# A fifth exponent buffer, half the descriptor scratch, and one product moved ahead of the last attention values

## The chip, the core and the metric

The program runs on one core of a Trainium2 chip. A core has five engines that run their own instruction streams and meet through semaphores: TensorE (PE, with weight loads shown as PEld), VectorE (DVE), ScalarE (ACT), GpSimd (POOL) and SyncE (SP, which only issues transfers). The metric is the device time of one execution in microseconds, lower is better. Small differences matter here: about 0.2% of the time is what a measurement of this kernel can tell from no change.

## The reference

The computation is a soft-capped attention followed by a mixture of experts with one expert per token.

```
scores = scale * np.matmul(q, k.transpose(0, 1, 3, 2))      # 8 batches, 12 heads, 448 x 64
scores = cap * np.tanh(scores / cap)
attn = np.exp(scores); attn = attn / attn.sum(-1)
x = (attn @ v).transpose(0, 2, 1, 3).reshape(3584, 768)
expert = argmax(x @ w_gate)                                 # one of 8 for each token
out[token] = gate * relu(x[token] @ w1[expert]) @ w2[expert]
```

## The kernel before

**Attention.** The work is cut into 24 quads (8 batches of 3 quads; a quad is 4 heads), each quad into 7 tiles of 64 keys, and two tiles make a step, so there are 84 steps. In step k PE makes the scores of tiles 2k and 2k+1 into PSUM tiles `sp` (L255, two buffers). ACT takes a tanh of each into one half of an exponent tile `pt` (L265), and one step later makes the exponent of the whole tile in place (`expo`, L272). Three steps after the scores PE multiplies the exponents with the values into PSUM tiles `po` (`pv`, L322; `values` decides which tiles). DVE adds the exponents up for the denominators (`adds`, L277, into `acc` and then `p4`; `p4` shows as p in the trace), and when a quad is complete it copies its two `po` tiles to SBUF (`outp`, L329, tile `ot`). A quad has two `po` tiles and there are two buffers in all, so the first value product of a quad waits for the copies of the quad before. A quad has 7 tiles and a step has 2, so every other quad ends on the first tile of a step; then the second tile's value product is held back to the next step (`held`).

**What follows a batch.** Three steps after a batch's last step PE makes the sums of `p4` (`sums`, L349), later the gate logits (L349 too, from `ot`), the spread of the reciprocals (L398), and the counts of the routing (L430, L491, L493); DVE does the small steps between (`st`, `rec`, `lt`, `lr`, `ob`), and POOL stores rows and token lists in DRAM (`xd`, `ids`).

**The early block.** When three batches are routed, a first block of 448 tokens (block number -2) is collected during attention: POOL gathers its rows `xg` (L745), DVE scales (L890) and transposes them (L901, tile `xt`), POOL splits each of the six 128-row pieces into a high part `xh` (L908) and a low part `xl` (L909), and the first weight chunks are split too. Its first product, `up_mm(-2, 0)` (L940, 18 matmuls, PSUM tile `ph`), stands behind the last scores. `ph` lies in the PSUM banks that the score tiles `sp` had.

**Experts.** After attention, 8 blocks of tokens follow the early one: six large ones (448 tokens) and two small ones. For each, PE makes the products with w1 (`up`, L940) and w2 (`down`, L975 and L983); POOL gathers the rows of the next block and scatters those of the last one with indirect transfers (L745, L755), two weight chunks of each kind included.

**Order.** The order on each engine is written out by hand: the step loop, a table of tasks by step (`at`, `do`), and the code behind the loop. Every engine runs its instructions strictly in that order. Tiles come from pools with a number of buffers; an instruction that writes a buffer again waits for the last readers of it. The transfers that POOL issues need descriptors in an SBUF scratch of `RING` bytes in each partition; pool `pb` (which holds `pt`) is placed behind it, and some tiles of the later pool `hw` reuse the space of `pb`.

The end of attention is this code:

Of the kernel before, what the change touches and what calls it, by code (L numbers as in the profile page):

```python
# [4 lines left out]
F32 = mybir.dt.float32  # L5
# [10 lines left out]
B, H, S, D = 8, 12, 448, 64  # L16
# [7 lines left out]
QB = S // 32  # L24


RING = 4096
QN = 11
QR = QB - QN

# [96 lines left out]
def attention_moe(tc, qT, kT, vL, capd, wgL, w1a, w1b, w2a, w2b, cst, cmk, out):  # L127
# [13 lines left out]
    pb = pools("pb")  # L141
# [103 lines left out]
    pts = {}  # L245
# [14 lines left out]

    def tanh(t):
        if t % 2 == 0:
            pts[t // 2] = pb.tile([128, 2, 2, S], F32, name="pt", bufs=4)
        scale = qsc if t < KT else 1.0
        A.activation(out=pts[t // 2][:, t % 2], in_=sps.pop(t)[:, :, 0:S], func=AF.Tanh, scale=scale)  # L265

# [4 lines left out]
    def expo(k):  # L271
        A.activation(out=pts[k], in_=pts[k], func=AF.Exp, scale=capt)  # L272
# [40 lines left out]
    def pv(t):  # L313
        m, g = divmod(t, KT)
        vr = vrs[m]
        if g == 0:
            pvs[m] = [ps_o.tile([128, 512], F32, name="po", bufs=2) for _ in range(2)]
        pt = pts[t // 2][:, t % 2]
        for c in range(2):
            for j in range(2):  # L320
                r, w = slice(64 * c, 64 * c + 64), slice(64 * j, 64 * j + 64)
                PE.matmul(  # L322
                    pvs[m][c][w, 0:S], vr[r, g, j, :], pt[r, j, :], start=g == 0, stop=g == KT - 1
                )
# [412 lines left out]
    def width(j):  # L737
        return LARGE if large(j) else SMALL
# [65 lines left out]
    def high(i, f, e=A):  # L804
        w, r = ((w1s, w1r), (w2s, w2r))[i - 1]
        (e.copy if e is A else e.tensor_copy)(out=w[f][0], in_=r[f // 4][:, f % 4, :])
# [122 lines left out]
    def up_mm(j, f, r=None):  # L929
        r = r or slice(0, width(j))  # L930
        xh, xl = m["xh"], m["xl"]
        wh, wl = w1s[f]
        if (j, f) not in phs:
            phs[j, f] = m["ps_h"].tile([128, 512], F32, name="ph")[:, 0 : width(j)]
        ph = phs[j, f][:, r]
        i = 0
        for k in range(KC):
            c = slice(128 * k, 128 * k + 128)
            for w, x in ((wh, xh), (wh, xl), (wl, xh)):
                PE.matmul(ph, w[:, c], x[:, k, r], start=i == 0, stop=i == 3 * KC - 1)  # L940
                i += 1
# [154 lines left out]
    for k in range(KC):  # L1096
        t = n_first + 24 + 3 * k
# [17 lines left out]
    def values(k):  # L1115
        nonlocal held
        last = None
        ready = held + [2 * k - 6, 2 * k - 5]
        held = [ready.pop()] if ready[-2] % KT == KT - 1 else []
        for t in ready:  # L1120
            pv(t)
            if t % KT == KT - 1:
                last = t // KT
        return last

    for k in range(STEPS):
        for n in range(QUADS - 2):
            if k == (KT * (n + 1) - 1) // 2 + 1:
                load(n + 2, 1)
                if n + 3 < QUADS:  # L1130
                    load(n + 3, 0)
        for t in (2 * k, 2 * k + 1):
            scores(t)
            tanh(t)
        do(k, "act")
        if k >= 1:
            expo(k - 1)
        if k >= 3:
            last = values(k)
            if last is not None:  # L1140
                outp(last)
        do(k, "pe1")
        do(k, "v0")
        if k >= 2:
            adds(k - 2)
        do(k, "v1")
        do(k, "v")
        if k == STEPS - 3:
            room()
            split_w1(1, G, G)  # L1150
# [3 lines left out]
    m["ps_h"] = pools("ps_h", bufs=2, space=PSUM, side="right", **tw)  # L1154
    m["ps_z"] = pools("ps_z", space=PSUM, side="right", **tw)
    expo(STEPS - 1)
    assert values(STEPS) is None
    up_mm(-2, 0)
    high(1, 2)
    low(1, 2, G)  # L1160
    adds(STEPS - 2)
# [289 lines left out]
```

## Time and profile before

| | us |
|---|---|
| median of 3 runs | 805.44 (804.15 to 806.04) |
| the profiled execution | 804.61 |
| its span, first to last instruction | 802.7 |
| PE busy in the span | 780.4 (97%) |
| DVE, ACT and POOL busy | 551.7, 449.4 and 411.4 |

The profiled execution is 1.9 us longer than its span, and 0.8 us shorter than the median of the runs. A busy PE is not a PE at its peak, since matmuls overlap and their ends are modelled.

### The profile page before, as it was taken

The page shows a single profiled execution, that of the slowest core. Times are in us where ns is not written, and L with a number is a line of the kernel's source. Part 1 is how long each engine was busy: PE and PEld are TensorE (multiplying, and loading weights), DVE is VectorE, ACT ScalarE, POOL GpSimd, SP SyncE. Part 2 cuts the span into 40 slices and gives each one's busy share as a digit, 9 for nine tenths or more (in the row PEclk, how much of TensorE's full clock was granted, in tenths as well). Part 3 has the DMA queues.
Part 4 walks back from the last instruction along what each step waited for, and adds up shares of the span by engine and source line. Part 5 has one row for each costly group of instructions (what it writes and reads, how often), then busy time and mean ns, then how long its engine had stood idle before and what let it go on. Part 6 is the DMA issues. An engine that isn't in the chain of part 4 may idle for free.

```text
span 802.7 us, 15069 instructions
## 1 busy us (share of the span) xinstructions
PE 780.4 (97%) x5984; PEld 571.4 (71%) x5984; DVE 551.7 (69%) x908; ACT 449.4 (56%) x534; POOL 411.4 (51%) x400
## 2 busy tenths in 40 slices
PE   8999999999999989999999999999999999999995
PEld 3343434343434436899999999999999999999995
DVE  2788897998899997878549448358347357357730
ACT  7999999999998992343334324224224233234520
POOL 1001330318474465353785784884884884764742
PEclk9999999999999999999999999999999999999998
DMA  8325573488879602493441133542510252454211
GB/s 283 102 107 162 118 210 129 116 228 208 236 171 254 187 17 58 81 345 112 165 172 41 51 109 140 212 135 109 218 50 31 67 183 98 173 190 165 71 57 52
DMA packets 37102, 112.62 MB, mean 140 GB/s; under 512 B 8609, under 2 KB 15699, under 8 KB 34464
## 3 DMA queue, kind: packets, MB, share of 16 engines
q0 software_dynamic: 18528, 63.93, 25.5%
q1 hardware_dynamic: 18208, 47.43, 19.0%
q8 instruction: 49, 0.80, 0.4%
q10 hardware_dynamic: 288, 0.23, 0.1%
q14 instruction: 29, 0.24, 0.1%
HBM read 101.69 MB, written 22.85 MB: 155 GB/s over the span
## 4 chain that ended last, share of the span: by engine, by line
PE 81%; ACT 7%; DVE 6%; issue 2%; POOL 2%; DMA 1%; POOLq 0%; DVEq 0%; ACTq 0%
PE ph L940 29%; PE y L975 22%; PE po L322 10%; PE sp L255 10%; PE y L983 4%; ACT pt L265 4%; ACT pt L272 3%; PE ms L349 2%; DVE acc L277 2%; POOL xg L745 1%; PE po L975 1%; PE z L975 1%; PE ms L975 1%; DMA xg<-xd,xi 1%; DVE ot L329 1%
## 5 line engine op out<-in xcount | busy, mean ns | idle before, releaser
L952 ACT ACTIVATE hb<-ph 128x448 fp32r<-128x448 f32 (+1 forms) x69 | 35.0, 508 | 264.1 <-PE ph L940 263.4
L745 POOL DMA_INDIRECT xg<-xd,xi x114 | 139.7, 1225 | 36.4 <-issue 27.0
L953 DVE SCALAR_TENSOR_TENSOR hb<-ph,hb 128x448 fp32r<-128x448 f32 (+1 forms) x69 | 39.5, 572 | 168.7 <-ACT hb L952 168.7
L255 PE MATMUL sp<-qk 64*64 64x448 f32 x1344 | 147.5, 549 | 5.3 <-ACT pt L265 5.2
L272 ACT ACTIVATE pt<-pt,capt 128x1792 f32<-128x1792 f32 x84 | 152.4, 1816 | 0.0
L265 ACT ACTIVATE pt<-sp 128x896 f32<-128x896 f32 x161 | 140.0, 934 | 16.4 <-DVE acc L277 6.8
L322 PE MATMUL po<-pt,vr 64*64 64x448 f32 x1344 | 144.5, 541 | 4.4 <-DVE ot L329 4.4
L755 POOL DMA_INDIRECT out<-ys,xi x98 | 104.4, 1066 | 27.3 <-issue 27.3
L322 PEld LDWEIGHTS po<-pt,vr 64*64 64x64 f32 x1344 | 54.0, 134 | 79.2 <-issue 69.0
L255 PEld LDWEIGHTS sp<-qk 64*64 64x64 f32 x1344 | 43.9, 132 | 82.0 <-ACT pt L265 57.3
L277 DVE TENSOR_TENSOR acc<-acc,pt 128x1792 f32<-128x1792 f32 (+1 forms) x36 | 61.5, 1707 | 4.1 <-ACT pt L272 4.1
L485 POOL DMA_DIRECT2D xd<-w2r x12 | 8.4, 710 | 104.8 <-DVE mx L456 104.6
L940 PE MATMUL ph<-xh,qk 128*128 128x448 f32 (+2 forms) x228 | 60.5, 340 | 0.0
L277 DVE TENSOR_TENSOR acc<-pt 128x896 f32<-128x896 f32 (+1 forms) x36 | 51.4, 1428 | 11.0 <-ACT pt L272 10.7
L516 POOL DMA_INDIRECT ids<-tokg,slots x32 | 43.5, 1360 | 25.6 <-DVE slots L510 16.5
L908 ACT CAST xh<-xt 128x448 fp32r<-128x448 f32 (+2 forms) x54 | 25.8, 490 | 33.5 <-DVE xt L901 33.5
L745 POOL DMA_INDIRECT w1r<-in_w1b,widx x7 | 10.5, 1495 | 66.4 <-DVE w17l L811 66.4
L940 PEld LDWEIGHTS ph<-xh,qk 128*128 128x128 f32 x228 | 40.8, 188 | 3.4 <-issue 0.7
L940 PE MATMUL ph<-xl,qk 128*128 128x448 f32 (+2 forms) x114 | 38.6, 339 | 0.0
L329 DVE COPY ot<-po 128x448 f32<-128x448 f32 x48 | 27.5, 614 | 15.5 <-PE po L322 15.4
L901 DVE STREAM_TRANSPOSE xt<-xg 128x448 f32<-128x448 f32 (+2 forms) x60 | 32.4, 549 | 1.4
L890 DVE TENSOR_TENSOR xg<-xg,sc 128x448 f32<-128x448 f32 (+2 forms) x60 | 30.2, 551 | 0.3
(368 smaller groups left out, 1789.9 us busy)
## 6 DMA issues: line engine op xcount, KB each, us to landing
vr<-in_vL SPq DMA_DIRECT2D x24, 448.0 KB, 4.9
qk<-in_qT SPq DMA_DIRECT2D x23, 448.0 KB, 5.9
qk<-in_kT SPq DMA_DIRECT2D x22, 448.0 KB, 5.8
xd<-yt POOLq DMA_DIRECT2D x16, 346.5 KB, 6.3
xd<-w2r POOLq DMA_DIRECT2D x12, 346.5 KB
w1r<-in_w1a SPq DMA_DIRECT2D x8, 384.0 KB, 7.1
w1r<-in_w1b SPq DMA_DIRECT2D x8, 384.0 KB, 8.0
w2r<-in_w2b SPq DMA_DIRECT2D x8, 384.0 KB, 8.8
```

The costliest lines, as they stand in the source:

```text
L255: PE.matmul(sp[w, r, 0:S], kr[h, c, 64 * g : 64 * g + 64], qr[h, c, :], start=True, stop=True)
L265: A.activation(out=pts[t // 2][:, t % 2], in_=sps.pop(t)[:, :, 0:S], func=AF.Tanh, scale=scale)
L272: A.activation(out=pts[k], in_=pts[k], func=AF.Exp, scale=capt)
L277: V.tensor_tensor(out=o, in0=a, in1=b, op=ALU.add)
L322: PE.matmul(pvs[m][c][w, 0:S], vr[r, g, j, :], pt[r, j, :], start=g == 0, stop=g == KT - 1)
L329: V.tensor_copy(out=ot, in_=pvs[m][c][:, 0:S])
L516: i = G.indirect_dma_start(out=ids, out_offset=bass.IndirectOffsetOnAxis(ap=slots[0:p, c : c + 1].bitcast(U32), axis=0), in_=tokg[0:p, c, ...
L745: G.indirect_dma_start(out=dst, out_offset=None, in_=src, in_offset=bass.IndirectOffsetOnAxis(ap=idx.bitcast(U32), axis=0), bounds_check=b ...
L755: i = G.indirect_dma_start(out=dst, out_offset=bass.IndirectOffsetOnAxis(ap=idx.bitcast(U32), axis=0), in_=src, in_offset=None, bounds_che ...
L940: PE.matmul(ph, w[:, c], x[:, k, r], start=i == 0, stop=i == 3 * KC - 1)
L953: V.scalar_tensor_tensor(out=hl, in0=ph, scalar=0.0, in1=hh, op0=ALU.max, op1=ALU.subtract)
L975: PE.matmul(y[k][:, 0:LARGE], w[:, c], h, start=f == 0 and i == 0, stop=f == FC - 1 and i == 2)
```

## The change

There are three edits. `RING` goes from 4096 to 2048. The exponent tiles get five buffers of 7168 bytes in each partition instead of four. And the early block's first product is written ahead of the value products of step 84.

```
-RING = 4096
+RING = 2048
...
-            pts[t // 2] = pb.tile([128, 2, 2, S], F32, name="pt", bufs=4)
+            pts[t // 2] = pb.tile([128, 2, 2, S], F32, name="pt", bufs=5)
...
     expo(STEPS - 1)
+    up_mm(-2, 0)
     assert values(STEPS) is None
-    up_mm(-2, 0)
     high(1, 2)
```

The moved product changes the order on PE alone, at the end of attention. The rows below are PE's, in the program before and then in the changed one; `sp` is the last step's scores, `po` the value products, `ph<-xh,w10h` and its kin the early block's first product, and a wait in brackets names the engine whose semaphore is waited for.

```order
L255 MATMUL sp<-qk 64x448 x3
L322 MATMUL po<-pt,vr 64x448 x4
L322 MATMUL po<-pt,vr 64x448 [waits DMAHW6_49,DVE_49]
...
L322 MATMUL po<-pt,vr 64x448 x7
L940 MATMUL ph<-xh,w10h 128x448 [waits Activation_49,Pool_49]
L940 MATMUL ph<-xl,w10h 128x448 [waits Pool_49]
...
L322 MATMUL po<-pt,vr 64x448 [waits Activation_49]
```

```order
L255 MATMUL sp<-qk 64x448 x3
L322 MATMUL po<-pt,vr 64x448 x4
L940 MATMUL ph<-xh,w10h 128x448 [waits Activation_49,Pool_49]
L940 MATMUL ph<-xl,w10h 128x448 [waits Pool_49]
...
L940 MATMUL ph<-xh,w10l 128x448
L322 MATMUL po<-pt,vr 64x448 [waits DMAHW6_49,DVE_49]
...
L322 MATMUL po<-pt,vr 64x448 x9
L322 MATMUL po<-pt,vr 64x448 [waits Activation_49]
```

Only the four value products of tile 160, which end quad 22, are left ahead of the 18 matmuls; the twelve of tiles 161 to 163, the first of which waits for DVE's copy of quad 22, now stand behind them. Twelve `ph` rows are left out in each list; each of the six pieces has its own wait for POOL's `xh` and `xl`.

On ACT the larger pool `pb` moves a wait. The rows are ACT's behind the last exponents, before and then after; `w13h` is a weight chunk of pool `hw`, `hb` the first rectified product of the early block.

```order
L272 ACTIVATE pt<-pt,capt 128x1792 [waits Activation_49] x2
...
L806 CAST w13h<-w1r_117 128x768 [waits DVE_49,DMAHW0_49,PE_49,Activation_49]
L952 ACTIVATE hb<-ph 128x448 [waits DVE_49,PE_49]
L952 ACTIVATE hb<-ph 128x448 [waits PE_49]
```

```order
L272 ACTIVATE pt<-pt,capt 128x1792 [waits Activation_49] x2
...
L806 CAST w13h<-w1r_117 128x768 [waits DMAHW0_49,DVE_49,PE_49]
L952 ACTIVATE hb<-ph 128x448
L952 ACTIVATE hb<-ph 128x448 [waits PE_49]
```

The copy `w13h` now stands in space that the last exponent tile uses, so it waits for the last value product and the last add, as `hb` did before; `hb` needs no wait of its own any more. DVE, POOL and SP issue the same instructions in the same order.

## Rows read from the trace of the kernel before

**Rows 1.** The page: PE's busy time, and shares of the chain that ended last.

```profile
PE 780.4 (97%) x5984; PEld 571.4 (71%) x5984; DVE 551.7 (69%) x908; ACT 449.4 (56%) x534; POOL 411.4 (51%) x400
PE 81%; ACT 7%; DVE 6%; issue 2%; POOL 2%; DMA 1%; POOLq 0%; DVEq 0%; ACTq 0%
```

**Rows 2.** Busy time by stretch: PE, PEld, DVE, ACT, POOL, then clock.

```profile
135.85:173.49 37.64, 36.57 (x433) 15.20 (x429) 36.49 (x69) 35.06 (x33) 10.82 (x9) 1.00 0.61 160
235.34:302.12 66.78, 61.67 (x730) 26.77 (x722) 64.41 (x94) 60.58 (x57) 32.77 (x25) 1.00 0.56 149
501.70:560.30 58.60, 58.60 (x290) 54.05 (x289) 33.04 (x51) 19.19 (x31) 40.02 (x42) 1.00 0.44 156
```

**Rows 3.** ACT's waits in 20 to 302 us: total, times, longest.

```profile
ACT pt L265 <- DVE acc L277: 6.8, 5, 1.9
ACT pt L265 <- PE po L322: 6.6, 11, 1.6
```

**Rows 4.** ACT's timeline: start, length, instruction, idle time before it.

```profile
67.89 1.73 ACT L265 ACTIVATE pt<-sp 128x896 f32<-128x896 f32 x2 [1.36 <-DVE acc L277]
...
171.28 1.79 ACT L272 ACTIVATE pt<-pt,capt 128x1792 f32<-128x1792 f32 x1
172.96 1.72 ACT L265 ACTIVATE pt<-sp 128x896 f32<-128x896 f32 x2
174.55 1.81 ACT L272 ACTIVATE pt<-pt,capt 128x1792 f32<-128x1792 f32 x1
177.08 1.73 ACT L265 ACTIVATE pt<-sp 128x896 f32<-128x896 f32 x2 [0.72 <-PE po L322]
```

**Rows 5.** DVE's timeline, where it idles and where it ends the sums' input.

```profile
88.17 2.02 DVE L277 TENSOR_TENSOR acc<-pt 128x1792 f32<-128x1792 f32 x1 [1.27 <-ACT pt L272]
...
158.63 1.09 DVE L277 TENSOR_TENSOR p<-acc 128x896 f32<-128x896 f32 x1
...
236.09 2.03 DVE L277 TENSOR_TENSOR acc<-pt 128x1792 f32<-128x1792 f32 x1 [0.75 <-ACT pt L272]
```

**Rows 6.** PE's timeline at one start of a step and one set of sums.

```profile
75.56 1.79 PE L255 MATMUL sp<-qk 64*64 64x448 f32 x16 [0.69 <-ACT pt L265]
...
159.43 1.74 PE L349 MATMUL ms<-p,cs 128*32 128x352 f32 x24
```

**Rows 7.** The chain that ended last, merged: start, length, what.

```profile
276.26 2.25 PE po L322 x24
...
302.76 4.19 PE po L322 x24
306.94 3.86 PE ph L940 x18
310.80 3.17 PE po L322 x32
```

**Rows 8.** End of attention: timelines of PE, ACT, DVE and POOL.

```profile
298.48 0.93 PE L322 MATMUL po<-pt,vr 64*64 64x448 f32 x8
...
299.10 1.74 ACT L265 ACTIVATE pt<-sp 128x896 f32<-128x896 f32 x2
...
302.12 1.12 DVE L329 COPY ot<-po 128x448 f32<-128x448 f32 x2
...
302.90 1.15 POOL L909 TENSOR_TENSOR xl<-xt,xh 128x448 fp32r<-128x448 f32 x1
...
311.56 1.09 DVE L277 TENSOR_TENSOR p<-acc 128x896 f32<-128x896 f32 x1
```

**Rows 9.** Stretches there; behind POOL's column the granted clock.

```profile
303.00:305.00 2.00, 2.00 (x12) 1.16 (x14) 2.00 (x3) 1.91 (x2) 1.06 (x2) 0.50 0.14 41
306.00:308.00 2.00, 2.00 (x16) 1.19 (x8) 1.97 (x4) 0.00 (x0) 1.45 (x2) 1.00 0.00 0
```

**Rows 10.** POOL's gathers: durations in ns, and landing times in us.

```profile
L745 POOL DMA_INDIRECT xg<-xd,xi x114: 992/1032/2598, 181.9 to 746.1; - x114
...
DMA to landing us min/median/max: 2.7/3.5/7.9
```

## The prediction

> **What bounds the kernel now.** I read the page first, then the busy time by stretch, then the waits and timelines of the stretches that the edits touch. PE is busy 780.4 of 802.7 us and 81% of the chain that ended last is PE's [rows 1]: time is won only where PE itself waits, or where it works slowly. In a large expert block PE is busy 58.60 of 58.60 us, while POOL works 40.02 us of it [rows 2]. Nothing in this change touches PE's work there, so from about 320 us on the kernel should only move as a whole, unless POOL falls behind.
>
> In attention no engine rules alone. ACT's free pace is 3.28 us a step: two tanh and one exponent, with the exponent's successor starting 1.68 us after it, as from 171.28 to 172.96 [rows 4]. PE needs about 3.0 us for the eight groups of matmuls of a step (its 24 value products take 2.25 us [rows 7], a third of that for each tile, and four tiles' worth make a step), and more in steps with sums or logits. DVE is the one that is easy to overlook: from 135.85 to 173.49 it is busy 36.49 of 37.64 us, and the rest is the few hundredths between its 69 instructions; from 235.34 to 302.12 it is 64.41 of 66.78, with 94 instructions [rows 2]. In such stretches an earlier ACT gives nothing, since the sums, the copies of `po` and the routing come from DVE. ACT's waits that a spare exponent buffer can end are 6.8 us on DVE's adds (five times) and 6.6 us on PE's value products (eleven times) [rows 3]; they are the two readers of the buffer that tanh wants to overwrite.
>
> **The fifth buffer.** With five buffers a tanh waits for readers of five steps ago, not four. Both kinds of wait end at their place: the held tile's value product, which is late by a step, is no longer asked for, and DVE may be a whole step later. What PE and DVE let through of these 13.4 us is the question. The stalls repeat with a period of two batches (21 of the 84 steps that end at 302 us, so some 75 us), because every other quad ends on the first tile of a step. I go through one period.
>
> The stall of the adds (67.89, 1.36 us [rows 4]) is followed by 0.69 us in which PE has no sp to write [rows 6]. In the first period DVE has room behind it: it idles 1.27 us at 88.17 [rows 5]. So the gain there is between 0.69 and 1.36; I take 1.0, the middle. In the second and third period DVE is full at that place: the sums at 159.43 need the `p4` that DVE ends at 158.63 + 1.09 = 159.72 [rows 5, 6], so PE would reach the sums sooner and wait. Nothing there, except that in the third period DVE's own wait for an exponent at 236.09, 0.75 us [rows 5], ends because ACT is ahead by then: 0.75.
>
> The stall of the held tile comes in three places of a period. One, in the middle of the first batch of a period, lies in a stretch where PE follows with sums and logits without a pause, so ACT only waits for scores a little later: nothing. One lies inside DVE's full stretch: nothing. The third is at 177.08, and ACT's cadence would have begun that tanh at 174.55 + 1.68 = 176.23 [rows 4]: 0.85. It lies just behind DVE's full stretch, which ends at 173.49 [rows 2]; I take it that ACT sets the pace from there until the next sums, so that it stays won. It occurs before 235 us twice: 1.7. Its third occurrence falls into the full stretch from 235.34 on [rows 2].
>
> Sum: 1.0 + 1.7 + 0.75 = 3.45, say 3.5 us. The bounds are nothing (DVE takes it all) and the whole 13.4 us. The other waits of ACT are for scores, which this edit does not bring sooner.
>
> **The moved product.** PE ends tile 160 at 299.4 and then waits until 302.76 for DVE's copy of quad 22, which starts at 302.12 [rows 7, 8]; behind that it works at a granted clock of 0.50, the lower level of 1.2 GHz, and is back at 1.00 from 306 on [rows 9]. The 24 value products after the wait took 4.19 us where others take 2.25 [rows 7]. So the wait costs twice.
>
> In the new order the 18 matmuls stand first. Their PSUM bank needs the first tanh of the last step (299.10 + 0.87 = 299.97 [rows 8], about a microsecond sooner with the fifth buffer), so 15 of them, at 3.86 / 18 = 0.21 us each [rows 7], run within the old wait. The sixth piece needs `xl`, which POOL ends at 302.90 + 1.15 = 304.05 [rows 8]; this is the new wait, and queued behind it are the last two matmuls and all value products that are left. The product then ends at 304.5. The value products begin 1.7 us later than before, but PE has worked in between and stands still at most a microsecond or so, so I take the full clock: 304.5 + 2.25 = 306.75, where they ended at 306.94 before. From there the 3.86 us of the product are gone [rows 7]. Gain 3.86 + 0.19 = 4.05, say 4.0. If the clock falls all the same, they end at 304.5 + 4.19 = 308.7 and the gain is 2.1.
>
> What is late next: the sums now want `p4` at 306.75 + 3.17 + 3.86 = 313.8 [rows 7] instead of 317.8, and DVE has it at 311.56 + 1.09 = 312.65 [rows 8]. It holds, by 1.1 us. `w13h` on ACT now waits for the last add, just ahead of that `p4`; `hb` stands behind it, and DVE's half of `hb` behind its copies of quad 23. The third product needs `hb` only after the sums and logits, so I put this at nothing too; its price, should it be late, would be about the microsecond by which `p4` has room.
>
> The Trainium skill ("TensorE: Matmul & The Clock Gate", Part 1) says that idleness throttles TensorE to half its clock and sustained work releases it; the trace agrees, 0.50 after the wait. By that rule alone a shortened idle time leaves the clock up, and the sum is the one above.
>
> **The scratch.** POOL's transfers get half the descriptor space, and the order of its instructions does not change. The price is nothing as long as POOL never waits for space. What speaks for that: a gather takes 1032 ns in the median and 2598 at most, although landings take 3.5 us in the median and up to 7.9 [rows 10], so two to six are in flight and the issue does not slow down. What hides a small delay is POOL's idle time of 18.6 us in a block [rows 2]. No row shows a full scratch, so the upper bound is the rival below.
>
> The Trainium skill ("DMA: Bandwidth & Descriptors", SWDGE vs HWDGE vs iDMA) says that GpSimd writes such descriptors into rings in SBUF, from which the transfer engines drain them. That speaks against this edit: by it a smaller ring could make GpSimd wait for landings. No run here shows one full.
>
> **Sum.** 804.61 - 3.5 - 4.0 = 797.1 for an execution like the profiled one. That one is 0.8 us below the median of the runs, so I put the median of the changed kernel at 797.5, between the two.
>
> **The rivals.**
> - *DVE swallows the buffer.* The 3.5 us are lost at the next copy or sum, and only the moved product is left: 804.6 - 4.0 = 800.6. For it speaks how full DVE is [rows 2]; against it that it idles at 88.17 and 236.09 for ACT [rows 5].
> - *The clock falls at the end anyway.* PE waits too long for the sixth piece: 804.6 - 3.5 - 2.1 = 799.0. With both of these, 802.5.
> - *ACT's waits all come back.* If DVE's full stretches only look full because its adds share time with POOL, all 13.4 us of [rows 3] return: 804.6 - 13.4 - 4.05 = 787.2. Against it speak the sums that wait for `p4`.
> - *Slower: the scratch runs full.* The median landing of 3.5 us against an issue of 1.0 [rows 10] means that several transfers must fit. In a block some 34 gathers and scatters share POOL's idle 18.6 us [rows 2]; I allow 0.3 us before each for plain issue, an estimate, so 18.6 - 10 = 8.6 us are free, 0.25 us for each. From there on the block lasts longer: at 0.35 us each by 34 x 0.1 = 3.4 us, six times, 20 us, which less the gains gives 817.
> - *No effect.* The new waits (for `xl` and for the add ahead of `w13h`) take back what is won: about 805.
>
> **Chances.** About 0.2% of the time, 1.6 us, is what a measurement of this kernel can tell from no change. The forecast, between 794.5 and 800: 0.50. Only the moved product: 0.17. The low clock: 0.08. All of ACT's waits or most: 0.10. Slower through the scratch or something like it: 0.10. No effect: 0.05. The range is 791.5 to 803.5, which leaves out the far end of ACT's case and the last two. Faster by over 0.2%: 0.50 + 0.17 + 0.08 + 0.10 = 0.85; within 0.2% 0.05; slower 0.10.
>
> **What would show it.** Right: ACT waits no more for DVE's adds or PE's value products before a tanh; the idle time moves to scores, and DVE's full stretches keep their length. DVE starts the copy of quad 22 near 298.6, 3.5 us sooner. The 18 matmuls stand between tile 160 and tile 161 and the clock stays at 1.00. From the sums on everything is 7.5 us earlier, the blocks still last 58.6 us. Wrong: a clock of 0.50 between 299 and 304; a copy of quad 22 at 302; POOL's gathers with means well over 1.2 us, or PE with waits inside a block.

## The result, and the profile after

| | before | after |
|---|---|---|
| median, us | 805.64 (804.15 to 806.87, 5 runs) | 796.68 (795.93 to 797.34, 5 runs) |
| profiled execution and its span, us | 804.61, 802.7 | 796.68, 794.9 |

The ratio is 0.9888 with a 95% interval of 0.9874 to 0.9902: 1.1% less, against 797.5 us forecast. The page of the changed kernel, with PE's busy time and the shares of the chain that ended last, answers to [rows 1].

```profile
PE 778.3 (98%) x5984; PEld 580.5 (73%) x5984; DVE 550.9 (69%) x908; ACT 448.8 (56%) x534; POOL 414.6 (52%) x400
...
PE 84%; DVE 11%; ACT 3%; issue 2%; POOL 0%; POOLq 0%; DVEq 0%
```

ACT's waits from 20 to 302 us answer to [rows 3] (total, times, longest):

```profile
ACT pt L265 <- PE sp L255: 13.5, 18, 1.6
```

Both kinds of wait on the buffer's readers are gone, 13.4 us of them, and ACT now waits for scores instead, as the forecast said it would.

The end of attention, by the timeline of PE, then of DVE, then of POOL, answers to [rows 7, 8]:

```profile
296.23 0.93 PE L322 MATMUL po<-pt,vr 64*64 64x448 f32 x8
...
301.84 0.47 PE L940 MATMUL ph<-xl,w10h 128*128 128x448 f32 x1 [0.75 <-POOL xl L909]
...
302.45 5.49 PE L322 MATMUL po<-pt,vr 64*64 64x448 f32 x56
```

```profile
299.87 1.12 DVE L329 COPY ot<-po 128x448 f32<-128x448 f32 x2
```

```profile
300.65 1.14 POOL L909 TENSOR_TENSOR xl<-xt,xh 128x448 fp32r<-128x448 f32 x1
```

(A value product counts twice in these rows: the four of tile 160 are the x8, and the twelve of tiles 161 to 163 are x24.) The last values of tile 160 start at 296.23 where they started at 298.48, 2.25 us sooner. DVE's copy of quad 22 moves by the same, from 302.12 [rows 8] to 299.87; the forecast had put it near 298.6. The product stands behind them, PE waits 0.75 us for the sixth piece's `xl` (and 0.21 for its `xh`), and the 56 value products follow in one piece. Two stretches of that place and one large block, with the columns of [rows 2]:

```profile
302.00:305.00 3.00, 3.00 (x30) 1.27 (x34) 2.93 (x6) 0.00 (x0) 2.42 (x1) 1.00 0.00 0
...
495.50:554.10 58.60, 58.60 (x289) 54.05 (x289) 33.00 (x51) 19.19 (x31) 39.84 (x41) 1.00 0.44 156
```

The granted clock stays at 1.00 where it was 0.50 [rows 9], and the block lasts 58.60 us as before [rows 2], with POOL at 39.84 where it was 40.02. The chain that ended last, in order of time, has the rest of the tail:

```profile
302.52 5.42 PE po L322 x56
307.94 3.87 PE ph L940 x18
311.81 2.54 PE ms L349 x24
```

The sums stand at 311.81, where they stood right behind the second product at 313.97 + 3.86 = 317.83 (the row at 310.80 in [rows 7] ends at 313.97, and the product takes 3.86): 6.02 us sooner, of which 2.25 came from attention and 3.77 from the tail.

That leaves 7.8 - 6.0 = 1.8 us of the span's gain, and they lie at the very end. This is POOL's last transfer in the kernel before, with the answer's first line, which gives the span:

```profile
core 0 of [0], span 802.7 us
...
794.93 0.97 POOL L755 DMA_INDIRECT out<-ys,oi  x1 [2.09 <-DVE ys L1015]
```

and this in the changed kernel:

```profile
core 0 of [0], span 794.9 us
...
789.07 0.97 POOL L755 DMA_INDIRECT out<-ys,oi  x1 [1.83 <-DVE ys L1015]
```

From the start of that scatter to the end of the span it was 802.7 - 794.93 = 7.77 us, and is 794.9 - 789.07 = 5.83: 1.94 us that no step of the prediction had. Between the sums and this scatter nothing was won: 794.93 - 317.83 = 477.10 and 789.07 - 311.81 = 477.26.

### The profile page after: what moved, and what is told of

Its sections match the earlier page's. It is cut to its first block, busy times and chain, and to the rows that moved or that the text cites. A ratio compares the mean times of both kernels' runs of the same rounds, so it can differ in the third digit from the quotient of the medians.

```text
span 794.9 us, 15050 instructions
## 1 busy us (share of the span) xinstructions
PE 778.3 (98%) x5984; PEld 580.5 (73%) x5984; DVE 550.9 (69%) x908; ACT 448.8 (56%) x534; POOL 414.6 (52%) x400
## 4 chain that ended last, share of the span: by engine, by line
PE 84%; DVE 11%; ACT 3%; issue 2%; POOL 0%; POOLq 0%; DVEq 0%
PE ph L940 29%; PE y L975 22%; PE sp L255 11%; PE po L322 11%; PE y L983 4%; DVE acc L277 3%; PE ms L349 3%; ACT pt L265 2%; DVE p L277 2%; PE z L975 1%; PE po L975 1%; PE ms L975 1%; ACT pt L272 1%; DVE ot L329 1%; DVE yt L340 1%
## 5 line engine op out<-in xcount | busy, mean ns | idle before, releaser
L272 ACT ACTIVATE pt<-pt,capt 128x1792 f32<-128x1792 f32 x84 | 154.2, 1837 | 0.0
L265 ACT ACTIVATE pt<-sp 128x896 f32<-128x896 f32 x161 | 141.9, 957 | 13.7 <-PE sp L255 13.5
L322 PEld LDWEIGHTS po<-pt,vr 64*64 64x64 f32 x1344 | 58.0, 133 | 70.6 <-issue 59.1
L255 PEld LDWEIGHTS sp<-qk 64*64 64x64 f32 x1344 | 49.1, 132 | 72.2 <-issue 34.3
L516 POOL DMA_INDIRECT ids<-tokg,slots x32 | 45.5, 1422 | 26.1 <-DVE slots L510 16.7
```

The source lines that it names most:

```text
L255: PE.matmul(sp[w, r, 0:S], kr[h, c, 64 * g : 64 * g + 64], qr[h, c, :], start=True, stop=True)
L322: PE.matmul(pvs[m][c][w, 0:S], vr[r, g, j, :], pt[r, j, :], start=g == 0, stop=g == KT - 1)
L516: i = G.indirect_dma_start(out=ids, out_offset=bass.IndirectOffsetOnAxis(ap=slots[0:p, c : c + 1].bitcast(U32), axis=0), in_=tokg[0:p, c, ...
```

## The experiments

The experiments ran on four chips: the first four on one, the next four on a second, the three after them on a third, the last on a fourth. Each kernel was timed beside runs of the kernel before on the same chip, whose median was 805.3 to 806.6 us.

### One part at a time

**The product alone.** Of the three edits only this one:

```
     expo(STEPS - 1)
+    up_mm(-2, 0)
     assert values(STEPS) is None
-    up_mm(-2, 0)
```

> Only the early block's first product is moved; four exponent buffers and 4096 bytes of scratch stay. Theory of the prediction: the wait of 3.34 us is filled and the clock stays at 1.00, 4.05 us less, so a median near 801.6 against 805.6, and the last stretch after POOL's last scatter stays 6.8 us. Rival, the clock falls all the same: 2.1 us less, 803.5, with a granted clock near 0.50 between 302 and 305. Rival, the new wait for xl takes it back: no change.

Measured: 800.85 us against 805.31, ratio 0.9950 (0.9935 to 0.9965). The chain in order of time:

```profile
304.16 0.67 PE ph L940 x2
304.84 5.42 PE po L322 x56
310.26 3.87 PE ph L940 x18
314.13 2.54 PE ms L349 x24
```

Sums at 314.13 instead of 317.83 are 3.70 us, with a granted clock of 1.00 from 302 to 305. So the first theory holds and the low-clock rival falls. The sixth piece ends a little later than forecast (304.84, where I had 304.5).

**The buffer, and the scratch.** Two kernels: the changed one with the product put back, and the one before with only `RING = 2048`. They differ in the fifth buffer alone.

```
-            pts[t // 2] = pb.tile([128, 2, 2, S], F32, name="pt", bufs=4)
+            pts[t // 2] = pb.tile([128, 2, 2, S], F32, name="pt", bufs=5)
```

> Five exponent buffers and 2048 bytes of scratch, the product where it was. Theory from the trace after the change: attention ends 2.2 us sooner, nothing of it comes back in the tail, and the stretch after the last scatter is 1.9 us shorter through the scratch, so 4.1 us less, near 801.5. The prediction's size: 3.5 us from attention alone, 802.1, with a last stretch of 6.8 us. Rival, DVE swallows the buffer: tile 160 ends its products near 299.4 as before, and only the last stretch is shorter, 803.7 or, without that, 805.6.

> Only the scratch is halved. Theory from the trace after the change: the 2 us between the last scatter and the end of the span that the forecast did not have come from the scratch, so the stretch after the last scatter falls from 6.8 to 4.9 us and the time is 1.9 us less, 803.7. Rival (the forecast's zero): the last stretch stays 6.8 us, no change, 805.6; then the 1.9 us are of another cause. Rival, the scratch fills up: gathers with means over 1.2 us, and a time over 807.

(These expectations, and those on the scratch below, count the last stretch from the scatter's end, 0.97 us behind its start.) Measured: 799.58 us with buffer and scratch, ratio 0.9934 (0.9920 to 0.9948), and 803.52 with the scratch alone, ratio 0.9979 (0.9969 to 0.9988). So the buffer is worth 3.9 us by these medians, and the scratch 1.8. Attention gave more than the 2.2 us that the first two profiles had let expect. This is PE's timeline with the scratch alone, the starts of the sums of five batches and the last values ahead of the tail (the rows with x21 and x23 are cut short by the window that was asked for):

```profile
85.68 1.41 PE L349 MATMUL ms<-p,cs 128*32 128x352 f32 x24
...
123.02 1.38 PE L349 MATMUL ms<-p,cs 128*32 128x352 f32 x21
...
159.49 1.75 PE L349 MATMUL ms<-p,cs 128*32 128x352 f32 x24
...
197.15 1.41 PE L349 MATMUL ms<-p,cs 128*32 128x352 f32 x24
...
233.62 1.61 PE L349 MATMUL ms<-p,cs 128*32 128x352 f32 x23
...
298.55 0.93 PE L322 MATMUL po<-pt,vr 64*64 64x448 f32 x8
```

and this with the fifth buffer too:

```profile
84.39 1.41 PE L349 MATMUL ms<-p,cs 128*32 128x352 f32 x24
...
120.88 1.41 PE L349 MATMUL ms<-p,cs 128*32 128x352 f32 x24
...
156.51 0.79 PE L349 MATMUL ms<-p,cs 128*32 128x352 f32 x4
157.53 1.40 PE L349 MATMUL ms<-p,cs 128*32 128x352 f32 x20 [0.24 <-DVE p L277]
...
194.01 1.41 PE L349 MATMUL ms<-p,cs 128*32 128x352 f32 x24
...
229.63 0.79 PE L349 MATMUL ms<-p,cs 128*32 128x352 f32 x4
230.71 1.40 PE L349 MATMUL ms<-p,cs 128*32 128x352 f32 x20 [0.29 <-DVE p L277]
...
294.78 0.93 PE L322 MATMUL po<-pt,vr 64*64 64x448 f32 x8
```

The starts are 1.29, 2.14, 2.98, 3.14 and 3.99 us sooner. But at 156.51 and 229.63 PE gets only four of the 24 matmuls through and then waits for `p4`: these two groups end at 158.93 and 232.11 instead of 161.24 and some 235.3, which is 2.3 and 3.2 us sooner. What a batch won has to be read between the ends of the sums, and so read three of these batches won some 0.83 us each, and the two that end with the wait 0.17 and nothing. The end of attention is 298.55 - 294.78 = 3.77 us sooner. The same batch in both kernels, the scratch alone and then with the buffer, by busy time in the columns of [rows 2]:

```profile
85.68:123.02 37.34, 37.34 (x442) 14.94 (x438) 32.16 (x48) 35.80 (x35) 9.37 (x11) 1.00 0.69 169
```

```profile
84.39:120.88 36.49, 36.49 (x440) 15.48 (x438) 32.19 (x48) 35.47 (x34) 12.16 (x11) 1.00 0.66 173
```

PE reads as busy for the whole batch in both, and yet the batch is 0.85 us shorter for the same work, so the busy row of the longer one holds waits, which the modelled ends of matmuls cover.

The stretch in which DVE is full [rows 2] lies between two copies of `po`. With four buffers and then with five they are these:

```profile
135.90 1.15 DVE L329 COPY ot<-po 128x448 f32<-128x448 f32 x2 [1.85 <-PE po L322]
...
174.20 1.16 DVE L329 COPY ot<-po 128x448 f32<-128x448 f32 x2 [0.65 <-PE po L322]
```

```profile
133.76 1.16 DVE L329 COPY ot<-po 128x448 f32<-128x448 f32 x2 [1.90 <-PE po L322]
...
171.90 1.16 DVE L329 COPY ot<-po 128x448 f32<-128x448 f32 x2 [0.66 <-PE po L322]
```

From one copy to the other it is 38.30 us with four buffers and 38.14 with five: the stretch moved as a whole and kept its length to 0.16 us.

### The closing stretch and the scratch

The changed kernel with 1024 bytes, and the kernel before with 8192:

> The changed kernel with the scratch halved once more, to 1024 bytes. If the last stretch follows the scratch in proportion, it gives another 1 us, 795.7 against 796.7. If it does not, 796.7. If the scratch is near full at 2048 bytes (the forecast's slower rival), gathers become slower than their 1.0 us median, PE waits inside the blocks, and the time is over 800.

> The kernel before with a scratch of 8192 bytes. The stretch behind the last scatter was 4.5, 4.9 and 6.8 us with 1024, 2048 and 4096 bytes. If it follows the scratch, it is 10 us or so here, and the time is some 3 to 4 us more, near 809. If it is the landing of the last transfers, and the scratch has nothing to do with it, no change: 805.3.

Measured: 796.37 us, ratio 0.9891 (0.9876 to 0.9906), and 807.17 us, ratio 1.0018 (1.0007 to 1.0030). The last scatter and the span, with 1024 and then with 8192 bytes:

```profile
core 0 of [0], span 793.9 us
...
788.42 0.97 POOL L755 DMA_INDIRECT out<-ys,oi  x1 [1.99 <-DVE ys L1015]
```

```profile
core 0 of [0], span 805.3 us
...
796.26 0.97 POOL L755 DMA_INDIRECT out<-ys,oi  x1 [2.08 <-DVE ys L1015]
```

From the scatter's start to the end: 5.48 us with 1024 bytes, 5.83 with 2048 (and 801.3 - 795.62 = 5.68 with the scratch alone), 7.77 with 4096 (and 798.9 - 791.23 = 7.67 with the product alone), 9.04 with 8192. The scatter is the same in all. So are the bytes that it moves: windows of half a microsecond show most of them between 1.5 and 2.5 us behind its start in all four sizes (a DMA share of 0.87 to 0.95, then of 0.65 to 0.75). What differs lies behind that, where no engine is busy and next to nothing is moved. The end of the program follows the size of the scratch, not in proportion: the step from 4096 to 2048 is worth 1.9 us, the next one 0.3 where 1 us was expected, and with 8192 bytes the time rose by 1.4 us and not by 3 to 4.

Two later runs with 1024 bytes came out otherwise; they stand last.

### The clock and the wait taken apart

The kernel before, with copies of the first product's matmuls in the wait:

```
     expo(STEPS - 1)
+    ph = phs[-2, 0] = m["ps_h"].tile([128, 512], F32, name="ph")[:, 0:LARGE]
+    for n in range(15):
+        PE.matmul(ph, w1s[0][0][:, 0:128], m["xh"][:, n // 3], start=n == 0, stop=n == 14)
     assert values(STEPS) is None
     up_mm(-2, 0)
```

> The kernel before, with 15 matmuls of the early block's first product issued a second time, ahead of the last quad's values, into the PSUM tile that the real product then starts over; nothing is moved, and PE does 3.1 us more work, inside its wait of 3.34 us. If the wait itself is what brings the low clock, the 24 value products behind it take about 2.25 us and not 4.19, and the time is some 1.9 us less, 803.4 against 805.3. If the clock falls for another reason, or the fall costs nothing, 805.3 and a granted clock of 0.50 between 302 and 305 as before.

Measured: 804.77 us against 805.77, ratio 0.9986 (0.9977 to 0.9995), so 1.0 us and not 1.9. PE's timeline:

```profile
301.20 3.27 PE L1159 MATMUL ph<-xh,w10h 128*128 128x448 f32 x15 [0.76 <-ACT pt L265]
304.40 2.49 PE L322 MATMUL po<-pt,vr 64*64 64x448 f32 x24
```

The 24 value products take 2.49 us where they took 4.19 [rows 7], and the clock is 1.00 from 302 to 305: PE did no useful work in the wait, and the clock stayed. So the wait itself costs the clock. The median shows 1.0 of these 1.7 us because the duplicates began 0.76 us late, behind the last tanh, and the value products now follow them and no longer DVE's copy: counted from the start of tile 160 (299.51 here, 298.48 before) they begin at 4.89 us and not at 4.28. The Trainium skill ("TensorE: Matmul & The Clock Gate", Part 1) says that idleness throttles the engine and sustained work releases it; this run agrees, since it differs in PE's work alone.

### Who bounds attention

Two kernels leave work out of the changed one, so their routing is another one and more expert blocks run; only their attention is compared, by the starts of the sums, with the changed kernel. DVE loses the second add into `p4` in twelve quads:

```
             add(p4, accs[m][:, 0], accs[m][:, 1])
-            add(p4, p4, pt[:, 0])
+            fill()
```

> The changed kernel without the second add into p4 in the twelve even quads: the denominators, and with them the routing, come out other than the reference's. DVE has 12 times 1.09 = 13.1 us less. If DVE bounds attention in its full stretches (the prediction), each of the four or five such adds there is won, 4 to 5 us, and the time is near 792. If PE bounds all of attention, only the tail moves, where the copy of quad 22 and xl come sooner and PE's two waits of 0.96 us end: near 795.7.

PE loses half of the logits (`strips` issues only its `h == 0` matmuls for them):

```
-    def strips(ps, operands):
+    def strips(ps, operands, halves=2):
...
         for (g, i, q0, q1, o), h in runs:
+            if h >= halves:
+                continue
```

> The changed kernel with half of the logits' matmuls left out (the logits miss half of the heads, so the routing differs from the reference's). PE has 8 times about 0.67 = 5.4 us less, DVE and ACT the same. If PE bounds all of attention, all of it is won: near 791.3. If DVE or ACT bound it, only the one batch behind attention's end moves, 0.7 us: near 796. If the bound changes by stretch, as the prediction had it (DVE full in 104 of 280 us), about 3 us: near 793.5.

The totals, 947.95 and 949.64 us, hold those further blocks and answer none of the expectations. In attention, from the same view of PE, batch by batch:

| sums to sums, us | 1 to 2 | 2 to 3 | 3 to 4 | 4 to 5 | 5 to 6 | 6 to 7 | last values of tile 160 |
|---|---|---|---|---|---|---|---|
| changed kernel | 35.62 | 36.49 | 35.64 | 38.14 | 35.99 | 39.97 | 296.23 |
| DVE less | 35.49 | 36.50 | 35.51 | 37.95 | 35.50 | 39.36 | 294.15 |
| PE less | 35.03 | 35.89 | 35.02 | 37.55 | 35.43 | 39.98 | 292.92 |

The rows behind the third line's first two entries and its last value are these:

```profile
49.04 1.41 PE L351 MATMUL ms<-p,cs 128*32 128x352 f32 x24
...
84.07 1.41 PE L351 MATMUL ms<-p,cs 128*32 128x352 f32 x24
...
119.96 1.41 PE L351 MATMUL ms<-p,cs 128*32 128x352 f32 x24
...
292.92 0.93 PE L322 MATMUL po<-pt,vr 64*64 64x448 f32 x8
```

Twelve logits matmuls less shorten each of the first five batches by 0.56 to 0.62 us, and the sixth by nothing. One or two adds of 1.09 us less in each batch shorten the first four by 0.2 or less, the fifth and sixth by 0.5 and 0.6. (By the ends of the sums the adds are worth 0.3, 0.0, 0.3 and 1.0 us in the last four, since PE waits inside two of these sums.) In sum PE's cut was worth 3.3 us of the 4.7 left out before the tail, DVE's 2.1 of some 12. So up to 230 us the logits left out had cost nearly their whole length, and the adds little; from there on it is the other way round. It does not follow that PE paces whole batches: each cut tells only of the steps in which it lies, and no run cut ACT's work. In ACT's timeline of the changed kernel, 54 of the 82 intervals from one exponent to the next (10 to 302 us) last 3.24 to 3.31 us, which is ACT's free pace of 3.27 us [rows 4], and the 0.6 us of the logits is won in a single interval of each batch.

### The changed kernel again, and two more versions

The changed kernel itself, and two versions in which DVE's two adds of quad 22's `p4` stand behind that quad's copies:

```
             if last is not None:
                 outp(last)
+            if k == STEPS - 1:
+                adds(k - 3)
...
-        if k >= 2:
+        if k >= 2 and k != STEPS - 2:
             adds(k - 2)
```

> The changed kernel once more. Its profiled execution started the last scores 2.3 us sooner than before, the two others with five buffers 3.7 and 3.5 us. If that is a difference between executions, the last scores start between 294.4 and 296 here too, and the median is 796 to 797. If the moved product costs attention something, they start near 295.9 again.

> The changed kernel with the two adds of quad 22's p4 moved on DVE from ahead of the last transpose xt and the copies of quad 22 to behind them. DVE is full there, so xt, and with it xh and xl of the sixth piece, and the copies come some 2.1 us sooner, and PE's two waits of 0.96 us end: near 795.7. If DVE is not what is late there, no change: 796.7.

> The same with 1024 bytes of scratch, whose last stretch was 0.3 us shorter than with 2048. Both together: 1.3 us less than the changed kernel, near 795.4. If neither holds, 796.7.

Measured, on one chip whose kernel before took 806.58 us: 797.20 (ratio 0.9888, 0.9867 to 0.9910), 796.02 (0.9872, 0.9852 to 0.9893) and 800.63 (0.9927, 0.9908 to 0.9945).

In the repeated run the last values of tile 160 start at 296.75, not at the 294.78 and 295.00 of the two runs on the first chip. Part of that is one short wait, on ACT at 185 us. It stands in the first profile of the changed kernel, and with 0.4 to 1.0 us at 183 to 189 us in every profile from the three later chips, four buffers or five, but in none of the four from the first of these chips. In the changed kernel's first profile:

```profile
185.56 0.92 ACT L265 ACTIVATE pt<-sp 128x896 f32<-128x896 f32 x1 [0.53 <-PE sp L255]
```

What causes it is open. It means that 2.25 us, the gain of attention between the two profiles shown first, compares executions with and without this wait, and the 3.77 us of two kernels on one chip is the better value of the buffer.

With the adds behind the copies, DVE's copies of quad 22 start at 297.80 and PE's product has no wait left:

```profile
297.80 1.12 DVE L329 COPY ot<-po 128x448 f32<-128x448 f32 x2
```

```profile
301.07 5.49 PE L322 MATMUL po<-pt,vr 64*64 64x448 f32 x56
```

This was the shortest of all, 1.2 us below the changed kernel on the same chip and with no run above 796.70 where that kernel's began at 796.71; the two ratios' intervals overlap, so its lead is not settled.

The version with 1024 bytes went the other way, 4.6 us longer. To see whether that is the scratch, the changed kernel with 1024 bytes ran once more:

> The changed kernel with 1024 bytes of scratch once more, since the version with 1024 bytes and late adds came out 4.6 us slower than the one with 2048, with waits near 198 and 210 us that the first run with 1024 bytes did not have. If 1024 bytes are at times too few, waits of a microsecond and more come in attention again and the median is near 800. If the slow one was due to its own order or to its place, the median is 796.4 again and the first three batches last 35.6, 36.5 and 35.6 us.

Measured on another chip: 800.94 us, ratio 0.9936 (0.9921 to 0.9950), where the first run had 796.37. ACT's timeline there:

```profile
207.97 1.79 ACT L272 ACTIVATE pt<-pt,capt 128x1792 f32<-128x1792 f32 x1
211.83 1.73 ACT L265 ACTIVATE pt<-sp 128x896 f32<-128x896 f32 x2 [2.08 <-remote]
```

Two of the three profiles with 1024 bytes have such a wait near 210 us, of 2.1 and 2.2 us; none with 2048 bytes does. In both, the profiled execution was the longest of its six (803.92 and 803.79), and what the others, at 799.59 to 801.39, waited for was not recorded. POOL's gathers are no slower with it: 1034 ns in the median and 2648 at most, as with 2048 bytes. So 1024 bytes are not safe, but that the scratch was full is not shown, and why ACT waits there stays open.

## Why the prediction was right, point by point

**What bounds the kernel.** The large blocks stayed at 58.60 us and the kernel moved as a whole from 320 us on: right. So was the picture of attention, in which no engine rules alone. "In such stretches an earlier ACT gives nothing" held for the stretch at 135.85 to 0.16 us (38.30 and 38.14 between its two copies): the sums began sooner and then waited for `p4`. DVE's hold on it was narrow, though. In the changed kernel without DVE's adds the steps behind these sums came only 0.3 us sooner, so what would bound the stretch next is that close.

**The fifth buffer.** Forecast 3.5 us, measured 3.9 by the medians and 3.77 by the profiles of two kernels that differ in nothing else. The mechanism was right, place by place. Here is what each batch won between the ends of the sums, with the scratch alone and with the buffer too, beside the forecast (the first sums start at 49.22 and 48.75, the seventh at 273.05 and 269.28):

| us | to the 1st sums | 1 to 2 | 2 to 3 | 3 to 4 | 4 to 5 | 5 to 6 | 6 to 7 | to the last values |
|---|---|---|---|---|---|---|---|---|
| forecast | 0 | 1.0 | 0.85 | 0 | 0.85 | 0 | 0.75 | 0 |
| measured | 0.47 | 0.82 | 0.85 | 0.17 | 0.83 | 0.01 | 0.62 | 0.00 |

The first stall of the adds was put at 1.0 and gave 0.8. The held tile's stall that was priced at 0.85 gave that twice, at 103 and 177 us. The one in the middle of the first batch of a period was put at nothing and gave nothing: with five buffers ACT waits for scores instead, a little later, as these rows show (the scratch alone, then with the buffer).

```profile
126.91 1.73 ACT L265 ACTIVATE pt<-sp 128x896 f32<-128x896 f32 x2 [0.64 <-PE po L322]
```

```profile
131.54 1.73 ACT L265 ACTIVATE pt<-sp 128x896 f32<-128x896 f32 x2 [0.83 <-PE sp L255]
```

At the second and third stall of the adds PE reaches the sums sooner and waits for `p4`, as forecast. What the forecast did not have is the start: 0.47 us ahead of the first sums, of which 0.17 stand already at the first exponents and are no work of the buffer.

That the batch from 85.68 got shorter although PE reads as busy for all of it is no contradiction. The Trainium skill ("Perfetto Trace Analysis", Identifying the Most-Contended Engine) says that a matmul's busy share is no good measure of how near TensorE is to its limit; the two windows of 37.34 and 36.49 us agree.

**The moved product.** Forecast 4.0 us, measured 3.70 with the product alone and 3.77 in the changed kernel's tail. Each step is in the trace: the 18 matmuls in the old wait, the new wait for `xl`, the clock at 1.00. The term that was a little off is the end of the product, 304.84 instead of 304.5. `p4` held: it was ready ahead of the sums, and they follow the second product without a wait. That the lower clock was a cost of the wait, and not of its place, is shown by the duplicated matmuls.

**The scratch.** "The price is nothing" held for the running program: gathers take 1031 ns in the median and 2766 at most, against 1032 and 2598 [rows 10]. But nothing was not the whole of it: the end of the program got 1.8 to 1.9 us shorter, and four sizes show that this is the scratch. The forecast's sum lacked this term altogether. The slower rival did not happen at 2048 bytes. Of the others, DVE took what the buffer gave in the places where the forecast had it take it, and not all, and ACT's 13.4 us of waits ended without coming back as time: ACT waits 13.5 us for scores instead.

**The sum.** In the profiled executions 2.25 + 3.77 - 0.16 + 1.94 = 7.80 us, the span's 802.7 - 794.9; the forecast was 3.5 + 4.0. That it came so near is in part luck: the missing 1.9 us of the scratch stood against 1.25 us that attention gave less than forecast in this execution, and 0.23 in the tail. The medians differ by 8.96. The parts timed singly, 4.46, 3.94 and 1.79, make 10.19 by their medians. By the ratios the product alone (0.50%) and buffer with scratch (0.66%) make 1.16% against 1.12% for all three, and each ratio's interval reaches some 0.15% to either side, so it is not shown that the parts differ from the whole.

The kernel before also scatters more than the one with the product moved. Its 17 runs on the first chip of the experiments took 803.25 to 806.15 us: three of them, at mean granted clocks of 0.996 and 0.997, took at most 803.75, and the other fourteen, at 0.993 to 0.995, took 804.76 and more. All five runs with only the product moved stand at 0.996 or 0.997. This is what one would see if the clock stayed up in some executions of the old order; only one execution of each kernel was profiled, so it is not shown.

## What to carry to other kernels

Where an instruction waits just ahead of independent work in its own queue, putting that work first can pay twice: the wait is filled, and the engine's clock does not fall behind it. A full busy row is no proof that an engine lets nothing through; compare the length of the same stretch in two kernels, or cut a little of each engine's work and see which steps that shortens. Read a gain behind a wait and not ahead of it: the starts of the sums showed gains that the wait for `p4` took back. And a resource's size can cost time at the very end of a program, where no wait points to it: look at the stretch behind the last transfer too.

## What the runs showed of the hardware that was not expected

- The time from the last scatter to the end of the program grows with the descriptor scratch: 5.48, 5.83, 7.77 and 9.04 us for 1024, 2048, 4096 and 8192 bytes.
- With 1024 bytes the same kernel took 796.37 us on one chip and 800.94 on another; the one profile there, of the longest run, has a 2.08 us wait of ACT in attention that has no visible cause.
- A wait of 0.4 to 1.0 us on ACT near 185 us stands in every profile from three chips and in none of the four from another, whatever the kernel; its cause is open.
